# A planner's constants and a written order, both replaced: one core, a linear-attention block beside a ReLU block

## The chip, the cores and the metric

The kernel runs on one core of one Trainium2 chip. The metric is the time of one execution on the device in microseconds (us), and lower is better. A kernel is run several times and the median counts. Beside it stands one profiled execution, whose records are the source of every row of a view shown here.

## What is computed

The input `x` has 2048 rows (tokens) of 640 numbers in bfloat16. Its rows are normalised, and the normalised rows go into two branches that meet in a product at the end.

```
xn = layernorm(x)
q, k, v = xn @ wqkv                     # wqkv 640 x 1920, 32 heads of 20
phi(t) = where(t > 0, t + 1, exp(t)) + 1e-6
kv = einsum("bhsd,bhse->bhde", phi(k), v);  z = sum over s of phi(k)
s  = (phi(q) kv) / (phi(q) z) @ wo      # wo 640 x 640
g  = silu(relu(xn @ w1) @ w2)           # w1 640 x 1728, w2 1728 x 640
out = x + s * g
```

## The kernel before

**Tiles.** The 2048 tokens are 16 tiles of 128. A tile of `x` is 128 x 640; `x_load` (L562) brings one in with 160 KB. The weights of the keys `wk` come in five pieces of 160 KB, one for each 128 rows (`wk_load`, L586), and `w1` in seven pieces, six of them of 320 KB (`w1_load`, L582), the query weights in one load of 800 KB (L567).

**The head.** For the tiles 0 to 3 the rows are centred on VectorE (L695, L699) and turned by TensorE against an identity (L706), copied out of PSUM (L716, L718), and multiplied by `wk` (`K_mm`, L733, two halves of 320 columns times five pieces, ten matmuls a tile). For the tiles 4 to 7 and again 0 to 3 the normalised rows (`bn`, L637, `aggr`, L641, the power on GpSimd, L645, `LN_norm`, L673) are turned by transfers: `xnT_dma` (L722) issues one transposing DMA for a tile on SP's queue. Blocks of `w1` for tokens 0 to 511 (`P4`, `P5`, `P10`, `P11`, L823, five matmuls of 512 columns each) need only what TensorE turned. The key tiles 4 to 7 (`KT4` to `KT7`) and the blocks `H14`, `H15`, `H110`, `H111` need the turned tiles 4 to 7.

**The units.** Nearly all other products are done in Strassen-like units of seven steps, s1 to s7, of two or three matmuls each (L1164 in the first two thirds, L991 in the rest). A unit's right sides are sums of turned tiles that VectorE makes. `T0` makes the five for tiles 0 to 7: `hTv[1]`, `hTv[3]`, `hTv[2]`, `hTv[4]` and `x4d`; each waits for all eight transposing transfers. The unit `a0` is the first to use them: `a0.s1` needs the eight turned tiles, `a0.s5` also `hTv[1]`, `a0.s6` also `hTv[2]`, and `a0.s7` also that VectorE has read the PSUM bank of `a0.s6` (the addition L936 with psT on both sides). Elementwise VectorE work of all kinds goes through one helper, `tt` (L936).

**Order.** `PROGRAM` is a text of words; each word is a step, and its place gives TensorE's and SP's order for certain. For the part ahead of the sign `|` (the head) it gives the order of every engine. After it, `Sched.place` picks for VectorE, ScalarE and GpSimd, from the next 60 operations of each, by the times that its own cost rules give. The constants `lags` are two delays that these rules add to the DMA queue, each as (time from which it counts, length). Waits are semaphores, put where one engine needs another's result. Words that the text uses: `lx5` loads tile 5, `lk12` loads piece 1 of `wk`, `lw4` loads piece 4 of `w1`, and `wb` is `w1` piece 4 as well; `S4` and `N4` are the statistics and the norm of tile 4 with its transposing transfer; `k012` multiplies tile 0 by piece 1 of `wk`; `tr3` turns tile 3; `pf3` is a filler matmul; `rb` is a scaling with one transposing transfer (L1051); `xa`, `xb`, `xc`, `lx8` load two tiles each, `lq` the query weights.

Of the kernel before, what the change touches and what calls it, by code (L numbers as in the profile page):

```python
# [95 lines left out]
class Sched:  # L96
# [90 lines left out]
    def place(self):  # L187
        recs = self.recs
        queue = {E: [o for o in recs if o.E == E] for E in ENGS}
        for o in recs:  # L190
            o.succ = []
        for o in recs:
            for d in o.deps:
                recs[d].succ.append(o.n)
        t = sum(o.occ for o in queue["PE"]) + 10.0
        end = t + 4.0
        goal = {}
        for o in reversed(queue["PE"]):
            t -= o.occ
            goal[o.n] = t  # L200
        for o in reversed(recs):
            o.late = min([recs[s].late - o.dur - self.LAT[o.E] for s in o.succ] + [goal.get(o.n, end - o.dur)])
        free = {E: 0.8 for E in ENGS}
        line = 2.0
        lags = [(3.8, 0.6), (13.0, 0.7)]
        narrow = turned = False
        nleft = [len(o.deps) for o in recs]
        ready = [0.0] * len(recs)
        wait = {E: list(queue[E]) for E in ENGS}
        left = sum(len(w) for w in wait.values())  # L210
        while left:
            best = None
            for E in ENGS:
                w = wait[E]
                if not w:
                    continue
                if E in ("PE", "SP") or w[0].n < self.head:
                    c = w[0]
                    if nleft[c.n]:
                        continue  # L220
                    est = max(free[E], ready[c.n])
                else:
# [130 lines left out]
m0.s1 n13 n10 m0.s5 p1.s7 m0.s6 p1.s3 m0.s2 p1.s4 m0.s7 n14 m0.s3 Kb8 m0.s4 n15 a1.s1 a1.s5 Ka12 p0.s1 p0.s5 y3 a1.s6 a1.s2 p0.s6  # L353
a1.s7 Ka8 a1.s3 T1 a1.s4 p0.s3 F5 a2.s5 a2.s1 y0 y8 y4 hh0 a2.s6 a2.s2 p0.s7 Ka11 a2.s7 p0.s4 p0.s2 a2.s4 a2.s3 y7 y1
k1.s1 y5 k1.s5 b0.s1 y6 Kb12 b0.s5 k1.s6 b0.s6 ZS y12 b0.s2 k1.s7 k1.s3 b0.s7 k1.s2 k1.s4 Kb15 y13 b0.s4 q0.s1 b0.s3 q0.s5 b1.s1
q0.s6 b1.s5 q0.s2 b1.s6 q0.s7 y2 q0.s3 b1.s2 q0.s4 b1.s7 b1.s3 k2.s5 k2.s1 b1.s4 Kb11 k2.s6 y9 a3.s5 a3.s1 k2.s2 k2.s7 k2.s3 a3.s6 a3.s2
k2.s4 Ka15 y14 y15 a3.s7 q1.s5 w2a q1.s1 a3.s3 a3.s4 q1.s6 q1.s2 GS0 b2.s5 y10 b2.s1 q1.s7 q1.s3 b2.s6 b2.s2 y11 q1.s4 b2.s7 GT1
zm SH2 zs c0 b2.s4 b3.s1 b3.s5 b2.s3 m1.s1 b3.s6 b3.s2 m1.s5 m1.s6 b3.s7 m1.s2 b3.s3 m1.s7 m1.s3 b3.s4 c1 sl w2b b4.s1 b4.s5
m1.s4 b4.s6 b5.s5 b4.s2 b5.s1 b4.s7 b4.s3 zc b5.s6 GT2 b5.s2 b4.s4 b5.s7 b5.s3 g0.s1 GT3 b5.s4 g0.s5 wo g0.s6 w2c hh1 GT4 dn
w2d g0.s7 g0.s3 do0 g1.s1 GS1 g1.s5 rc0 do1 g1.s6 g1.s2 uT1 g0.s2 g1.s7 g0.s4 do3 g1.s3 wv1 uT3 g1.s4 u0.s1 wv0 uSa0 uSb0  # L360
uT2 kv1 uT4 dv0 kv0 u0.s5 u0.s6 rc1 W5 W4 do2 u0.s2 u0.s7 uSa2 W1 u0.s3 W3 u0.s4 W2 W0 uSa1 uSb2 xre uSb1
u1.s1 u2.s1 dv1 u1.s5 u1.s6 u2.s5 rc3 u2.s6 u1.s3 u1.s7 dv3 oT u2.s7 oS0 uSa3 u2.s3 u2.s2 u2.s4 u1.s4 o0.s5 o0.s1 rc2 u1.s2 u4.s1
o0.s6 uSa4 u4.s5 u4.s6 uSb4 o0.s2 dv2 o0.s7 o0.s3 u4.s7 uSb3 oS1 o0.s4 u4.s2 o1.s5 u4.s4 o1.s1 u4.s3 u3.s1 o1.s6 u3.s5 oS2 uSa6 u3.s6
o1.s2 o1.s7 o1.s3 u3.s7 o1.s4 o2.s5 u3.s3 o2.s1 uSa5 u3.s4 u3.s2 oS3 uSb5 o2.s6 u5.s1 u5.s5 o2.s7 u5.s6 o2.s2 o2.s3 oS4 o2.s4 u5.s7 uSa7
o3.s5 o3.s1 u5.s2 o3.s6 o3.s2 u5.s4 o3.s7 o3.s3 u5.s3 o4.s1 o3.s4 u6.s5 o4.s5 o4.s6 o4.s2 u6.s1 o4.s7 e3 oS5 o4.s3 uSb6 u6.s6 o4.s4 u6.s2
o5.s5 oS6 o5.s1 u6.s7 u6.s3 o5.s6 u6.s4 o5.s2 o5.s7 o5.s3 e0 uSb7 o6.s1 o5.s4 o6.s5 u7.s5 o6.s6 u7.s1 o6.s2 o6.s7 u7.s6 o6.s3 o6.s4 u7.s2
u7.s7 u7.s3 e1 f0 f3 f1 u7.s4 l0 l1
"""


# [1611 lines left out]
```

## Time and profile before

| what | value |
|---|---|
| median of 3 runs | 202.93 us (202.88 to 203.06) |
| the profiled execution, its own time | 202.67 us |
| its span (first to last instruction) | 201.4 us |
| TensorE busy | 197.4 us, 98% of the span |
| VectorE, ScalarE, GpSimd busy | 172.1, 131.8, 42.5 us |
| granted TensorE clock | 1.00 |

The profiled execution took 1.27 us more than its span, and its own time is 0.26 us under the median. A view's row for an engine has the start, the length, the engine, the line, the operation, what is written and read, and in brackets the idle time ahead of it with what ended it. PE is TensorE, PEld its weight loads, DVE VectorE, ACT ScalarE, POOL GpSimd, SPq the issuing of SP's transfers. A matmul of 512 columns that follows another without a wait starts 0.216 us after it, one of 320 columns 0.136 us. A few matmul records are missing in the trace, so a gap of exactly one such step is no wait.

### The profile page before, as it was taken

To read this page: it belongs to the slowest core of one execution; us is meant where nothing else is said; L and a number is where in the kernel's file an instruction comes from. 1 tells how busy PE (TensorE), PEld (TensorE's weight loads), DVE (VectorE), ACT (ScalarE), POOL (GpSimd) and SP (SyncE) were. 2 spreads that over 40 slices of the span, in tenths; PEclk is the share of its full clock that TensorE was granted. 3 is DMA by queue.
4 is the path that set the end of the run, shared out by engine and by line. 5 is a ranking of instruction groups with operands and counts; after the bars stand their busy time and mean duration, and the time that the engine had idled before them with its cause. 6 is when DMAs were issued, how large, how long until landed. Compare 5 with 4: busy or idle time off the path is not lost.

```text
span 201.4 us, 3628 instructions
## 1 busy us (share of the span) xinstructions
PE 197.4 (98%) x1302; PEld 120.5 (60%) x1312; DVE 172.1 (85%) x408; ACT 131.8 (65%) x279; POOL 42.5 (21%) x66
## 2 busy tenths in 40 slices
PE   8999999999999999999999999999999999999995
PEld 3756444554564464545555777777777777777774
DVE  5899799999999979999574999999969977686565
ACT  6889858998999998867933313471636354654533
POOL 3489504143345605542000000000000000000000
DMA  5999798245567986685406965995993010111104
GB/s 155 331 279 111 110 370 182 44 98 103 112 146 138 184 203 130 134 165 97 131 0 206 306 164 167 276 268 132 352 358 131 0 65 0 68 67 65 38 30 130
DMA packets 38487, 30.43 MB, mean 151 GB/s; under 512 B 13765, under 2 KB 38469, under 8 KB 38469
## 3 DMA queue, kind: packets, MB, share of 16 engines
q1 hardware_dynamic: 32885, 23.62, 43.0%
q0 software_dynamic: 4624, 5.57, 14.1%
q10 hardware_dynamic: 960, 1.02, 1.6%
q8 instruction: 10, 0.16, 0.4%
q14 instruction: 8, 0.07, 0.1%
HBM read 15.81 MB, written 5.24 MB: 105 GB/s over the span
## 4 chain that ended last, share of the span: by engine, by line
PE 94%; DVE 2%; DMA 1%; issue 1%; ACT 0%; DVEq 0%
PE psT L991 43%; PE psT L1164 33%; PE psT L733 6%; PE psT L823 3%; PE psT L1494 2%; PE psT L605 2%; DMA reg<-reg 1%; PE psT L1838 1%; PE psT L841 1%; PE psT L706 1%; PE psT L1629 1%; PE psT L1603 1%; DVE regH L936 1%; DVE reg L761 1%; PE psT L895 1%
## 5 line engine op out<-in xcount | busy, mean ns | idle before, releaser
L1164 PE MATMUL psT<-reg 128*128 128x512 bf16 (+2 forms) x160 | 43.2, 370 | 0.5 <-issue 0.2
L991 PE MATMUL psT<-reg,regH 128*128 128x320 bf16 (+1 forms) x224 | 34.3, 299 | 0.0
L991 PE MATMUL psT<-reg 128*128 128x320 bf16 (+1 forms) x178 | 28.7, 299 | 0.0
L991 PEld LDWEIGHTS psT<-reg,regH 128*128 128x128 bf16 (+1 forms) x224 | 21.9, 98 | 8.5
L1164 PEld LDWEIGHTS psT<-reg 128*128 128x128 bf16 (+1 forms) x166 | 15.9, 98 | 18.2 <-DVE psT L936 0.7
L863 POOL DMA_DIRECT2D regH<-reg x16 | 18.4, 1192 | 21.6 <-DMA regH<-reg 6.3
L991 PEld LDWEIGHTS psT<-reg 128*128 128x128 f16 (+1 forms) x178 | 17.4, 98 | 7.1
L998 ACT ACTIVATE reg<-psT 128x320 f32<-128x320 f32 (+1 forms) x24 | 10.4, 436 | 17.0 <-PE psT L991 15.8
L936 DVE TENSOR_TENSOR reg<-reg 128x1024 f16<-128x1024 bf16 (+11 forms) x30 | 18.8, 648 | 1.5 <-ACT reg L1853 1.0
L1214 ACT ACTIVATE regH<-psT 128x512 bf16<-128x512 f32 (+1 forms) x24 | 14.9, 620 | 3.3 <-PE psT L1164 3.1
L991 PE MATMUL psT<-reg,pqT 128*128 128x320 bf16 (+1 forms) x84 | 15.8, 299 | 0.0
L1665 ACT ACTIVATE wv_sb<-psT 128x320 bf16<-128x320 f32 (+2 forms) x21 | 8.8, 424 | 9.2 <-PE psT L991 8.1
L936 DVE TENSOR_TENSOR psT<-psT,reg 128x320 f32<-128x320 f32 (+1 forms) x21 | 11.4, 543 | 3.7 <-PE psT L991 3.5
L1853 ACT ACTIVATE reg<-psT 128x640 bf16<-128x640 f32 (+1 forms) x14 | 7.8, 568 | 10.1 <-PE psT L991 10.1
L637 DVE BATCH_NORM_STATS2 stats<-reg 128x6 f32<-128x320 bf16 x28 | 12.4, 483 | 1.7 <-DMA reg<-in_A_x_dram 1.7
L733 PE MATMUL psT<-reg 128*128 128x320 bf16 x80 | 12.3, 299 | 0.0
L1171 ACT ACTIVATE psT<-psT 128x512 f32<-128x512 f32 (+1 forms) x18 | 10.6, 599 | 1.6 <-PE psT L1164 1.5
L936 DVE TENSOR_TENSOR reg<-psT,reg 128x320 bf16<-128x320 f32 (+1 forms) x16 | 7.8, 488 | 4.5 <-PE psT L991 4.5
L800 ACT ACTIVATE regE<-psT 128x512 bf16<-128x512 f32 x16 | 9.7, 604 | 3.0 <-PE psT L1164 2.8
L936 DVE TENSOR_TENSOR psT<-psT,wv_sb 128x512 f32<-128x512 f32 (+1 forms) x14 | 9.2, 654 | 2.8 <-PE psT L1164 1.9
L998 ACT ACTIVATE psT<-psT 128x320 f32<-128x320 f32 x17 | 7.3, 429 | 5.9 <-PE psT L991 5.9
L733 PEld LDWEIGHTS psT<-reg 128*128 128x128 bf16 x80 | 7.8, 98 | 4.2
(173 smaller groups left out, 404.3 us busy)
## 6 DMA issues: line engine op xcount, KB each, us to landing
regH<-reg POOLq DMA_DIRECT2D x16, 320.0 KB, 3.6
reg<-in_B_w_dram SPq DMA_DIRECT2D x12, 320.0 KB, 5.0
scr<-rden SPq DMA_DIRECT2D x4, 640.0 KB, 6.0
reg<-in_A_x_dram SPq DMA_DIRECT2D x4, 640.0 KB, 6.3
out_dram<-reg SPq DMA_DIRECT2D x14, 160.0 KB, 1.8
regE<-scr SPq DMA_DIRECT2D x3, 640.0 KB, 8.8
reg<-in_A_x_dram SPq DMA_DIRECT2D x4, 320.0 KB, 5.7
reg<-in_A_x_dram SPq DMA_DIRECT2D x7, 160.0 KB, 3.8
```

The source lines that it names most:

```text
L637: sc.op("DVE", lambda eng: eng.bn_stats(stats[:, t, a, :], xv[:, HN * a:HN * (a + 1)]), R=[("xin", xs(t))], W=[("stats", t, a)])
L733: fns.append(lambda eng, a=a, k=k, lhs=lhs: eng.matmul(ps[bk[a]][:, 0:HN], lhsT=lhs, rhs=wk[:, k, HN * a:HN * (a + 1)], start=(k == 0), st ...
L800: exps.append(sc.op("ACT", lambda eng: eng.activation(out=e_, in_=src, func=ACTF.Exp), R=[key], W=[("er_e", es)]))
L863: dma("POOL", lambda eng: eng.dma_start(zacc[a], src, **kw), R=[key] + after, W=[("zacc", a)], chain=zchain[a])
L936: sc.op("DVE", lambda eng: eng.tensor_tensor(out=out, in0=in0, in1=in1, op=op), R=R, W=W, extra=extra)
L991: sc.group("PE", [(lambda eng, k=k, lhs=lhs, rhs=rhs: eng.matmul(ps[b][:, 0:HN], lhsT=lhs, rhs=rhs, start=(start and k == 0), stop=(k == n ...
L998: sc.op("ACT", lambda eng: eng.activation(out=dst, in_=ps[b][:, 0:HN], func=ACTF.Copy), R=[("ps", b)], W=[dkey], extra=extra)
L1164: sc.group("PE", [(lambda eng, k=k, lhs=lhs, rhs=rhs: eng.matmul(ps[b][:, 0:nn], lhsT=lhs if tile is None else rhs, rhs=rhs if tile is Non ...
L1171: sc.op("ACT", lambda eng: eng.activation(out=dst[:, 0:nn], in_=ps[b][:, 0:nn], func=ACTF.Copy), R=[("ps", b)], W=[dkey], extra=extra)
L1214: sc.op("ACT", lambda eng: eng.activation(out=dst, in_=ps[b], func=ACTF.Relu), R=[("ps", b)], W=[("hT", j, f)], extra=ex)
L1665: sc.op("ACT", lambda eng, lo=lo, hi=hi: eng.activation(out=g[:, lo:hi], in_=src[:, lo - HN * n:hi - HN * n], func=ACTF.Silu), R=[key, ("s ...
L1853: sc.op("ACT", lambda eng: eng.activation(out=o_[:, 0:n].rearrange("p (a n) -> p a n", a=2) if n == D else o_[:, 0:n], in_=src, func=ACTF. ...
```

## The change

The second constant of `lags` goes from 13.0 us and 0.7 us to 18.2 us and 1.2 us, the first from 3.8 us to 4.1 us, and `PROGRAM` is replaced by another order of the same words but for the key weights of the head (the same forty key matmuls cut into other pieces), the engine of single copies, and `wb`, which stands ahead of `|` now. No operation is added or taken away. The head and the first units of both:

```
-        lags = [(3.8, 0.6), (13.0, 0.7)]
+        lags = [(4.1, 0.6), (18.2, 1.2)]
...
-lx0 ba0 mh0 lx2 lk01 ax1 lk12 lx3 ma0 ce0 lk23 lk34 lx4 lk45 ma1 lx7 ce1 ma2 tr0 cd0 pf3 bb0 tr1 k001
-ce2 sq1 ma3 lx6 lx5 cd1 ca3 lw5 k012 lw2 cd2 tr2 k102 ca5 k023 ba3 ag0 mh3 k034 cd4 k123 ce3 S4 sq2
-lw3 lw0 S7 tr3 k134 k045 k201 ca7 N4 S5 k212 k145 N2 ca6 k301 S6 k225 N5 ke0 ke1 bb3 N7 k312 ag3
-k325 SH0_1 mv6 kr0 kr1 ke2 N6 kr2 P11 P5 P10 ke3 N1 kr3 N0 N3 lq |
-lx8 F0 F3 F1 P4 lw6 xb SH0_2 S8 xa wa rb KT4 F2 KT5 KT7 SK KT6 H110 wb n8 F4 H15 n12
-SQ F7 a0.s1 F6 T0 SM a0.s5 SH0_4 SH0_3 H111 a0.s6 n11 H14 SH1 a0.s2 a0.s7 xc n9 p1.s1 a0.s3 p1.s5 a0.s4 p1.s6 p1.s2
...
+lx0 ba0 ax1 lx2 ma0 mh0 lk01 ma1 lx3 ce0 lk12 bb0 lk23 lx4 ce1 lk34 lk45 lx7 lx5 lw5 ag0 lw2 lx6 lw3
+ma2 ce2 lw0 wb tr0 pf3 ca0 sq2 tr1 cd1 ba3 ma3 k001 cd2 cd3 mh3 S4 tr2 k012 k023 ce3 S7 k103 k034
+ca4 ca5 k045 sq1 ke0 N4 k202 N0 tr3 bb3 k224 S5 N7 S6 ca6 SH0_1 ca7 k245 k135 N5 kr0 ke1 kr1 F1
+ag3 N6 N1 ke2 kr2 k301 k315 N2 P11 P10 F0 P4 P5 N3 lx8 lq ke3 SH0_2 lw6 kr3 F2 |
+S8 xb xa SH0_4 KT4 n8 wa F3 KT5 SH0_3 n12 rb n11 xc KT7 n10 F4 n13 KT6 SH1 n9 n15 F7 n14
+H14 SQ H111 a0.s1 SM H110 T0 T1 SK y3 a0.s5 a0.s6 a0.s2 H15 p1.s1 a0.s7 p1.s5 a0.s3 p1.s6 a0.s4 p1.s2 m0.s5 F6 m0.s1
...
```

The order that comes of it, read off the built programs: SP issues eleven tile and key loads, then `w1` pieces 5 and 2, tile 6, pieces 3, 0 and 4, and then the eight transposing transfers for the tiles 4, 0, 7, 5, 6, 1, 2, 3; before, twelve such loads (tile 6 among them) and four pieces of `w1` stood ahead of the eight, which went in the order 4, 2, 5, 7, 6, 1, 0, 3. After the eight come `lx8` and `lq` (before: `lq` and `lx8`). VectorE's share of `T0` is made in the order `x4d`, `hTv[3]`, `hTv[1]`, `hTv[2]`, then the statistics of tile 8, then `hTv[4]`; before, it was `hTv[1]`, `hTv[3]`, one addition for the keys, `hTv[2]`. On TensorE the 106th matmul, counted from the start, is one of `KT5` in both.

More of the change, by code (lines that the diff above doesn't have):

```diff
@@ L353 @@
[L353 to L364, printed above, removed]
@@ L365 @@
-o3.s5 o3.s1 u5.s2 o3.s6 o3.s2 u5.s4 o3.s7 o3.s3 u5.s3 o4.s1 o3.s4 u6.s5 o4.s5 o4.s6 o4.s2 u6.s1 o4.s7 e3 oS5 o4.s3 uSb6 u6.s6 o4.s4 u6.s2
-o5.s5 oS6 o5.s1 u6.s7 u6.s3 o5.s6 u6.s4 o5.s2 o5.s7 o5.s3 e0 uSb7 o6.s1 o5.s4 o6.s5 u7.s5 o6.s6 u7.s1 o6.s2 o6.s7 u7.s6 o6.s3 o6.s4 u7.s2
-u7.s7 u7.s3 e1 f0 f3 f1 u7.s4 l0 l1
+lx0 ba0 ax1 lx2 ma0 mh0 lk01 ma1 lx3 ce0 lk12 bb0 lk23 lx4 ce1 lk34 lk45 lx7 lx5 lw5 ag0 lw2 lx6 lw3
+ma2 ce2 lw0 wb tr0 pf3 ca0 sq2 tr1 cd1 ba3 ma3 k001 cd2 cd3 mh3 S4 tr2 k012 k023 ce3 S7 k103 k034
@@ new lines @@
+ca4 ca5 k045 sq1 ke0 N4 k202 N0 tr3 bb3 k224 S5 N7 S6 ca6 SH0_1 ca7 k245 k135 N5 kr0 ke1 kr1 F1
+ag3 N6 N1 ke2 kr2 k301 k315 N2 P11 P10 F0 P4 P5 N3 lx8 lq ke3 SH0_2 lw6 kr3 F2 |
+S8 xb xa SH0_4 KT4 n8 wa F3 KT5 SH0_3 n12 rb n11 xc KT7 n10 F4 n13 KT6 SH1 n9 n15 F7 n14
+H14 SQ H111 a0.s1 SM H110 T0 T1 SK y3 a0.s5 a0.s6 a0.s2 H15 p1.s1 a0.s7 p1.s5 a0.s3 p1.s6 a0.s4 p1.s2 m0.s5 F6 m0.s1
+p1.s7 y4 Kb8 m0.s6 p1.s3 p1.s4 m0.s2 m0.s7 F5 y7 Ka8 y8 a1.s1 a1.s5 m0.s4 m0.s3 a1.s6 Ka12 ZS p0.s1 a1.s7 p0.s5 p0.s6 a1.s2
@@ new lines @@
+a1.s4 a1.s3 y0 p0.s3 a2.s1 p0.s7 a2.s5 a2.s6 y6 hh0 p0.s4 y5 a2.s2 a2.s7 y1 Ka11 p0.s2 a2.s4 k1.s1 a2.s3 mv6 k1.s5 b0.s1 y2
+Kb12 b0.s5 k1.s6 b0.s6 y12 b0.s2 k1.s7 k1.s2 b0.s7 k1.s4 k1.s3 b0.s3 b0.s4 q0.s1 Ka15 y13 q0.s5 b1.s1 q0.s6 b1.s5 q0.s2 b1.s6 q0.s7 q0.s3
+b1.s2 q0.s4 y9 b1.s7 b1.s3 k2.s5 k2.s1 b1.s4 Kb11 y11 k2.s6 a3.s5 a3.s1 k2.s2 k2.s3 k2.s7 a3.s6 a3.s2 k2.s4 Kb15 y15 y14 a3.s7 q1.s5
+q1.s1 a3.s3 a3.s4 y10 q1.s6 GS0 w2a q1.s2 b2.s5 b2.s1 q1.s7 q1.s3 zm b2.s6 b2.s2 q1.s4 b2.s7 SH2 c0 m1.s1 b2.s4 GT3 zs m1.s5
@@ new lines @@
+m1.s6 b2.s3 GT1 m1.s2 b3.s1 m1.s7 b3.s5 m1.s3 b3.s6 c1 b3.s7 m1.s4 b3.s3 b4.s5 b3.s4 b4.s1 b3.s2 b5.s5 GT2 b5.s1 b4.s6 zc b4.s2 b5.s6
+b4.s7 b5.s2 b4.s3 b4.s4 b5.s7 b5.s3 g0.s1 b5.s4 w2b g0.s5 g0.s6 hh1 wo w2d w2c dn g0.s3 g1.s1 GS1 g1.s5 g1.s6 sl GT4 do0
+uT3 g0.s7 g1.s2 g1.s7 rc0 g0.s2 uSa0 uT2 g1.s3 dv0 g0.s4 wv0 uT1 do2 do1 uSb0 g1.s4 u0.s1 u0.s5 wv1 kv1 u0.s6 W5 uSa2
+W4 kv0 do3 u0.s2 u0.s3 uT4 W3 W1 u0.s7 W2 uSa1 u1.s5 u1.s1 u0.s4 W0 uSb1 u1.s6 u2.s1 rc2 u2.s5 u1.s7 oT u2.s6 u1.s2
+u1.s3 uSb2 uSa4 rc1 u2.s7 oS0 u1.s4 u2.s2 dv1 u2.s4 uSa3 xre o0.s5 rc3 o0.s1 u2.s3 u4.s1 o0.s6 u4.s5 oS1 u4.s6 o0.s2 uSb4 o0.s7
@@ new lines @@
+o0.s3 dv3 u4.s7 o0.s4 oS2 u4.s3 o1.s5 o1.s1 u4.s4 u4.s2 o1.s6 u3.s1 u3.s5 o1.s7 uSa6 uSb3 u3.s6 o1.s2 o1.s3 o1.s4 u3.s7 o2.s1 u3.s2 oS3
+o2.s5 o2.s6 u3.s4 o2.s2 u3.s3 uSa5 o2.s7 o2.s3 u5.s1 o2.s4 u5.s5 dv2 o3.s5 o3.s1 u5.s6 u5.s2 o3.s6 uSb5 u5.s7 o3.s2 o3.s7 u5.s3 oS4 u5.s4
+o3.s3 uSb6 oS5 o3.s4 e3 o4.s1 o4.s5 u6.s5 o4.s6 u6.s1 o4.s2 o4.s7 o4.s3 oS6 u6.s6 o4.s4 u6.s2 o5.s5 o5.s1 u6.s7 u6.s3 o5.s6 u6.s4 o5.s2
+uSa7 o5.s7 o5.s3 o6.s1 e0 o5.s4 o6.s5 u7.s5 uSb7 o6.s6 u7.s1 o6.s2 o6.s7 o6.s3 u7.s6 o6.s4 u7.s2 u7.s7 f0 f3 e1 u7.s3 f1 u7.s4
@@ L368 @@
+l0 l1
 """
```

## The prediction

> **What bounds the kernel now.** I read the page first, then the busy time by stretches, the chain of waits, and the timelines of TensorE, SP and VectorE up to 29 us.
>
> ```profile
> span 201.4 us, 3628 instructions
> PE 197.4 (98%) x1302; PEld 120.5 (60%) x1312; DVE 172.1 (85%) x408; ACT 131.8 (65%) x279; POOL 42.5 (21%) x66
> PE 94%; DVE 2%; DMA 1%; issue 1%; ACT 0%; DVEq 0%
> 26.43:61.36 34.93, 34.58 (x189) 17.18 (x194) 34.77 (x96) 31.40 (x67) 12.11 (x21) 1.00 0.58 139
> 61.36:198.82 137.46, 137.25 (x966) 89.18 (x970) 114.64 (x247) 78.22 (x171) 14.78 (x13) 1.00 0.54 145
> 61.36 0.38 PE L1164 MATMUL psT<-reg 128*128 128x512 bf16 x1 [0.19 <-issue]
> ```
>
> TensorE is the bound: 98% busy, 94% of the chain. Of the two stretches after 26.43 us (length, then busy time of PE) the one idles 0.35 us and the other 0.21 us, and one missing record of 512 columns, 0.216 us, accounts for the second and most of the first. That leaves the row at 61.36 us: its 0.19 us of idle, and, against 60.80 us plus two steps of 0.216 us, a wait of 0.13 us. So an order can win next to nothing after 26.43 us, and can only lose there. What it can win lies before:
>
> ```profile
> 22.69 1.24 PE L823 MATMUL psT<-reg 128*128 128x512 bf16 x5
> 24.00 0.59 PE L1164 MATMUL psT<-reg 128*128 128x512 bf16 x2
> 24.74 0.60 PE L1164 MATMUL psT<-regE,pqT 128*128 128x512 f16 x2
> 25.18 1.24 PE L823 MATMUL psT<-reg 128*128 128x512 bf16 x5
> 26.43 0.59 PE L1164 MATMUL psT<-regX,pqT 128*128 128x512 f16 x2
> 60.80 0.38 PE L1164 MATMUL psT<-wv_sb,reg 128*128 128x512 f16 x1
> 21.23 2.68 DMA reg<-reg
> 23.99 0.69 DVE L936 TENSOR_TENSOR regE<-reg 128x1024 f16<-128x1024 bf16 x1 [1.00 <-DMA reg<-reg]
> ```
>
> These are TensorE's starts around `a0`. At 0.216 us a step it could have begun `a0.s1` at 22.69 + 1.08 = 23.77 us and began at 24.00; `a0.s5` at 24.43, began at 24.74; `a0.s6` at 26.26, began at 26.43. The three waits are 0.23, 0.31 and 0.17 us, 0.71 us in all. The chain's DMA row says where they are from: the last of the eight transposing transfers, issued at 21.23 us, landed at 21.23 + 2.68 = 23.91 us, and VectorE, idle for a microsecond, began `T0` on it at 23.99. All of `a0` hangs on that landing.
>
> **The transposing transfers (the first and largest term).** What sets the landing is SP's timeline and the queue's rows.
>
> ```profile
> 6.45 3.36 SPq L582 DMA_DIRECT2D reg<-in_B_w_dram  x4
> L582 SPq DMA_DIRECT2D reg<-in_B_w_dram x7: 434/526/1453, 6.5 to 28.8; - x7
> 10.64 1.33 SPq L722 DMA_TRANSPOSE reg<-reg  x1
> 15.96 2.60 SPq L722 DMA_TRANSPOSE reg<-reg  x2
> 17.29 3.90 SPq L722 DMA_TRANSPOSE reg<-reg  x2
> 21.23 1.27 SPq L722 DMA_TRANSPOSE reg<-reg  x1
> q8 instruction: 1, 0.02, 3.8%
> 0.00:18.43 18.43, 17.55 (x105) 10.14 (x107) 15.24 (x48) 15.27 (x32) 11.29 (x31) 1.00 0.87 232
> GB/s 155 331 279 111 110 370 182 44 98 103 112 146 138 184 203 130 134 165 97 131 0 206 306 164 167 276 268 132 352 358 131 0 65 0 68 67 65 38 30 130
> 10.16 0.45 DVE L673 TENSOR_SCALAR reg<-reg,mv,rsy 128x640 bf16<-128x640 bf16 x1
> ```
>
> SP hands out one such transfer every 1.3 us (2.60 us for two), so eight take about 9.2 us from the first issue to the last. One pair takes 3.90 us, 1.30 more, and in the 2.8 us from 18.4 us on the queue view has one packet of 0.02 MB on the instruction queue, the first since the program began. So the landing is: first issue 10.64 + 9.24 + 1.35 lost + 2.68 = 23.91 us.
>
> The Trainium skill ("Runtime: NRT & Kernel Launch", section "Instruction fetch mechanics") says that an engine's instructions come in blocks of 16 KiB, 256 at a time, and that crossing a block is mostly hidden. TensorE shows no wait there, so for its own sequencer the trace agrees; for the queue beside it the 1.30 us of the pair disagree, and the measurement decides.
>
> The read can't be planned away by this change: it comes after 105 recorded matmuls, and the 106th is one of `KT5` in both orders, at a time when transposing transfers are still being handed out. I keep the loss at 1.35 us in both, with 0.3 us to either side, since it depends on which of a transfer's packets it hits.
>
> What moves is the first issue. Two things hold it. VectorE must have made the norm of tile 4: before at 10.16 to 10.61 us, after the statistics of tile 7. In the new order tile 4 arrives one place earlier and tile 7 in the same place, so these statistics start some 0.2 us earlier (they need not queue behind tile 4's), and the norm ends at about 10.3 us: 0.3 us earlier is the low end. The other is SP. It issued four pieces of `w1` in 3.36 us, where a short issue is 0.434 us and the longest took 1.453: the queue was full, and an issue ended when something had drained. It ended at 6.45 + 3.36 = 9.81 us, 0.83 us ahead of the first transposing one. The new order puts a fifth piece in between. 320 KB (327,680 bytes) drain in 1.07 us at some 305 GB/s, the mean of the second and third slice of the GB/s row (331 and 279, 5 to 15 us). So SP is free at 9.81 + 1.07 = 10.88, and the first issue comes at about 10.92 us, 0.28 us later than before. The high end has a row too:
>
> ```profile
> 25.87 2.84 SPq L1051 DMA_TRANSPOSE wv_sb<-spx  x1
> ```
>
> This transposing transfer was issued behind six loads and its issue alone took 2.84 us, 1.51 more than the 1.33 of the row at 10.64. If the first of the eight fares a third to two thirds as badly behind its longer line, that is 0.5 to 1.0 us more. I take +0.28 us, the term for which every number is a row of the same place, and keep -0.3 and +1.2 as ends.
>
> **The key phase of the head.** TensorE waits for pieces of `wk` in it.
>
> ```profile
> 6.12 0.11 PEld L733 LDWEIGHTS psT<-reg,regX 128*128 128x128 bf16 x2 [0.21 <-DMA reg<-in_A_wqkv_dram]
> 6.53 0.49 DVE L637 BATCH_NORM_STATS2 stats<-reg 128x6 f32<-128x320 bf16 x1 [0.28 <-DMA reg<-in_A_x_dram]
> 8.04 0.89 DVE L637 BATCH_NORM_STATS2 stats<-reg 128x6 f32<-128x320 bf16 x2 [0.21 <-DMA reg<-in_A_x_dram]
> 8.33 3.69 PE L733 MATMUL psT<-reg,regX 128*128 128x320 bf16 x26
> ```
>
> Piece 1 lands just before 6.12 us, tile 3 before 6.53, and three loads later tile 4 before 8.04, 0.50 us each. The new order gives tile 3 the place of piece 1 and tile 4 that of piece 3, so piece 3 lands at about 8.0 and piece 4 in its old place at 8.5 us. TensorE can't go on with `k045` before; with it and after it come 26 matmuls of 0.136 us, and the turning of tile 3, 0.28 us: 8.5 + 3.53 + 0.28 = 12.3 us, against 8.33 + 3.53 = 11.86 now. That is 0.44 us, and it is covered: up to `a0.s1` lie the same 30 matmuls of 512 columns and 40 of 320 in both, 11.9 us, so TensorE arrives at 24.2 instead of 23.77 us, and the landing, 23.91 + 0.28 = 24.19 us, is as late. Cost nothing; but it spends the cover. If the landing came early, 24.2 us would be the bound.
>
> **From the landing to `a0.s7`.** Here VectorE's order changes.
>
> ```profile
> 24.60 0.69 DVE L936 TENSOR_TENSOR regX<-reg 128x1024 f16<-128x1024 bf16 x1
> 26.20 0.42 DVE L936 TENSOR_TENSOR regX<-reg,pqT 128x512 f16<-128x512 bf16 x1
> 26.54 0.69 DVE L936 TENSOR_TENSOR regE<-reg,regX 128x1024 f16<-128x1024 bf16 x1
> 27.47 0.70 DVE L936 TENSOR_TENSOR psT<-psT,wv_sb 128x512 f32<-128x512 f32 x1
> 9.08 0.83 DVE L637 BATCH_NORM_STATS2 stats<-reg 128x6 f32<-128x320 bf16 x2
> ```
>
> Steps from start to start: 1024 elements 0.61 us (23.99 to 24.60), 512 elements 0.34 (26.20 to 26.54), a statistic 0.41. Counted from `T0`'s start D: `x4d` 0.34, `hTv[3]` and `hTv[1]` to 1.56, `hTv[2]` done at 1.56 + 0.69 = 2.25; before, it was done at 26.29, D + 2.30. So `a0.s6` can't start much before D + 2.4, as now (26.43 is D + 2.44), and the block of `H110` in the wait hides no more than that of `H111` did. Then come two statistics of tile 8, `hTv[4]`, about 0.8 us of small work with another statistic, and the addition that frees the bank for `a0.s7`: 2.17 + 0.82 + 0.61 + 0.8 = 4.4, done at D + 5.1. TensorE with no wait after `a0.s6` gets to `a0.s7` at 2.44 + 0.43 + 0.65 + 1.08 + 0.43 = D + 5.03. Before, the addition ended at 28.17 us and `a0.s7` came after it with room. So a wait of 0.1 us to 0.3 (should tile 8's load keep VectorE) is new; I take 0.15.
>
> **The rest.** Moves of the units, of copies, and of `wb` out of the later queue cost nothing as far as I can price them: TensorE hides them, with the waits gone or at 0.13 us. But VectorE is busy for 34.77 of the 34.93 us from 26.43 to 61.36, so a unit that moves up has nothing to lean on there. I put this at 0, from -0.13 (the wait at 61.36 gone) to +0.5 us (three or four waits of the size of that one).
>
> **The sum.** +0.28 (first issue) + 0.15 (`a0.s7`) + 0 = +0.43 us. On the profiled execution: 202.67 + 0.43 = 203.10 us. That execution lies 0.26 us under the median of the runs, 202.93, so on the scale of the medians it is 203.36, rounded to 203.4 us.
>
> **The rivals.**
>
> *The landing comes earlier (faster).* The queue doesn't hold SP at the fifth piece, the first issue follows the norm at 10.34 us, 0.3 earlier, or the instruction read falls into a pause between two transfers. Then TensorE is the bound, at 24.2 us for `a0.s1`; of the 0.71 us of waits 0.43 are spent in the key phase, and 0.3 us are won, 0.13 more if the wait at 61.36 us goes, and 0.6 in all if the key phase loses less than I think. For it: the norm is earlier. Against it: the 1.453 us issue. Time 202.3 to 202.6 us.
>
> *The first transposing issue is stretched (clearly slower).* Behind a full queue it takes 1.0 us longer, as the row of 2.84 us suggests. It decides from the point where the last landing passes 24.3 us, TensorE's arrival. Price +1.2 us with the rest: 204.1 us.
>
> *Nothing moves.* The landing stays within 0.1 us, since tile 6's load now stands between the pieces and leaves SP less held, and VectorE's order costs nothing: 202.8 to 203.1 us.
>
> *The middle gives way.* VectorE, full up to 61 us, makes new waits for the units: +0.5 us on top of the forecast, 203.9 us.
>
> **How the numbers follow.** About 0.2% (0.4 us) is what a measurement of this kernel can tell from no change. The forecast, slower by 0.2 to 0.6 us, gets 0.32; the stretched issue 0.13 and the middle 0.11; nothing moves 0.16; the early landing 0.28. The forecast's case reaches into "within 0.2%" with about a fifth of its chance, the early landing with 0.04 of its 0.28, which gives faster 0.26, same 0.22, slower 0.52. The range from 202.3 to 204.3 us takes in the ends of the first issue and of the middle.
>
> **What would show it right or wrong.** In the profile of the changed kernel: the first transposing issue at about 10.9 us behind five pieces of `w1` (wrong if at 10.4; the stretched case if its own length passes 1.8 us); one pair at 3.9 us beside an instruction packet; VectorE's first addition of `T0` near 24.3 us; the `P` blocks starting at about 12.3 us; a short wait of TensorE at `a0.s7` behind VectorE; no wait over 0.3 us after 30 us. A start of `a0.s6` before 26.3 us would make the forecast wrong.

## The result and the profile after

Six runs of the changed kernel have a median of 205.23 us (204.09 to 206.09), beside 202.91 us (202.52 to 203.37) for six of the kernel before on the same chip: a ratio of 1.0112, with 95% interval 1.0075 to 1.015. The change costs 2.3 us, where 0.43 was forecast; the time lies above the range. The profiled execution took 206.09 us, the slowest of the six, so its trace shows more loss than the median has.

From the page of the changed kernel: its span, TensorE's row, and the shares of the chain that ended last.

```profile
span 204.8 us, 3631 instructions
PE 199.0 (97%) x1312; PEld 119.2 (58%) x1312; DVE 172.6 (84%) x407; ACT 132.5 (65%) x280; POOL 37.7 (18%) x66
PE 76%; DVE 7%; DMA 6%; ACT 5%; SPq 3%; issue 2%; POOL 1%; DVEq 0%
```

TensorE's busy time is 1.6 us more than before, with ten more matmul records of the same work. Its share of the chain has gone from 94% to 76%: DMA, VectorE, ScalarE and SP's queue now hold stretches that were TensorE's own. (The chain runs along them also where TensorE is busy beside them; the lost time itself is read from TensorE's waits below.)

SP's timeline around the first transposing transfers (start, length, engine, line):

```profile
7.96 3.29 SPq L582 DMA_DIRECT2D reg<-in_B_w_dram  x3
10.27 0.99 SPq L582 DMA_DIRECT2D reg<-in_B_w_dram  x1
11.30 2.59 SPq L722 DMA_TRANSPOSE reg<-reg  x1
13.94 1.26 SPq L722 DMA_TRANSPOSE reg<-reg  x1
```

The first issue comes at 11.30 us, not 10.92, and takes 2.59 us, where the prediction put the mark of the stretched case at 1.8. The second starts at 13.94 us; before it started at 12.02. The chain has the last of the eight, TensorE's timeline what hangs on it:

```profile
21.86 4.09 DMA reg<-reg
```

```profile
19.34 4.23 PE L733 MATMUL psT<-reg 128*128 128x320 bf16 x30 [0.58 <-DMA reg<-reg]
26.04 0.59 PE L1164 MATMUL psT<-reg 128*128 128x512 bf16 x2 [0.30 <-DMA reg<-reg]
28.35 0.59 PE L1164 MATMUL psT<-regX,pqT 128*128 128x512 f16 x2
144.46 0.72 PE L991 MATMUL psT<-reg,regH 128*128 128x320 f16 x4 [0.89 <-DVE psT L936]
```

The last landing is at 21.86 + 4.09 = 25.95 us (23.91 before), `a0.s1` starts at 26.04 (24.00) and `a0.s6` at 28.35 (26.43): 1.92 us are lost by then. The row at 19.34 is new: `KT5` waits for tile 5, which is now transposed fourth and not third. So is the row at 144.46, which no step of the prediction has. The chain shows how it comes about:

```profile
137.72 0.50 SPq L1644
138.26 2.02 SPq L1644
140.33 2.74 DMA reg<-reg
143.51 0.48 DVE reg L936
143.99 0.42 DVE psT L936
144.46 0.58 PE psT L991 x3
```

L1644 stores the pieces of `wf`; the last lands at 143.07 us. VectorE's next instructions are the first two of `oT`, which need all of `wf`, and the addition that frees TensorE's bank stands behind them.

From `a0.s6` to the end of the last matmul the traces give 172.66 us before and 174.16 after. Of the 1.50 more, 1.05 are the wait that ends at 144.46 us. The other 0.45 are mainly short waits between 40 and 57 us (0.08, 0.12, 0.21 and 0.10 in the trace's steps), with the 0.13 us at 61 us gone.

### The profile page after: what moved, and what is told of

Same layout as the page of the kernel before. It is cut to its first block, busy times and chain, and to the rows that moved or that the text cites. A ratio compares the mean times of both kernels' runs of the same rounds, so it can differ in the third digit from the quotient of the medians.

```text
span 204.8 us, 3631 instructions
## 1 busy us (share of the span) xinstructions
PE 199.0 (97%) x1312; PEld 119.2 (58%) x1312; DVE 172.6 (84%) x407; ACT 132.5 (65%) x280; POOL 37.7 (18%) x66
## 4 chain that ended last, share of the span: by engine, by line
PE 76%; DVE 7%; DMA 6%; ACT 5%; SPq 3%; issue 2%; POOL 1%; DVEq 0%
PE psT L991 39%; PE psT L1164 26%; PE psT L733 4%; DMA reg<-reg 3%; DMA reg<-in_A_wqkv_dram 2%; PE psT L1494 2%; ACT pqT L802 1%; DVE stats L637 1%; SPq L1644 1%; PE psT L1838 1%; PE psT L841 1%; PE psT L823 1%; DVE reg L936 1%; ACT regE L800 1%; ACT regE L743 1%
## 5 line engine op out<-in xcount | busy, mean ns | idle before, releaser
L1164 PE MATMUL psT<-reg 128*128 128x512 bf16 (+2 forms) x166 | 44.7, 370 | 0.3 <-DMA reg<-reg 0.3
L1164 PEld LDWEIGHTS psT<-reg 128*128 128x128 bf16 (+1 forms) x166 | 15.8, 98 | 18.0 <-DVE psT L936 0.9
```

The costliest lines, as they stand in the source:

```text
L1164: sc.group("PE", [(lambda eng, k=k, lhs=lhs, rhs=rhs: eng.matmul(ps[b][:, 0:nn], lhsT=lhs if tile is None else rhs, rhs=rhs if tile is Non ...
```

## The experiments

Most edits move single records of the planner's order and leave every other engine's order as it is. They use one helper, at the end of the file:

```python
def moved(seq, recs, moves):
    for a, b in moves:  # record a goes right behind record b
        seq.remove(recs[a])
        seq.insert(seq.index(recs[b]) + 1, recs[a])
    return seq
```

All their results in one table. The landings, the start of `a0.s6` and the rest (from there to the end of the last matmul) are read from the trace of the profiled execution, in us; "last copy" is the latest landing among the loads that are issued ahead of the transposing ones. "Fifth piece" is the piece of `w1` that the change puts ahead of them.

| kernel | last copy | first / last transposed | a0.s6 | rest | this execution | median |
|---|---|---|---|---|---|---|
| before | 14.26 | 14.98 / 23.91 | 26.43 | 172.66 | 202.67 | 202.91 |
| before, again | 15.31 | 16.03 / 24.76 | 27.29 | 172.67 | 203.51 | 203.00 |
| after | 16.24 | 16.80 / 25.95 | 28.35 | 174.16 | 206.09 | 205.23 |
| after, fifth piece back | 15.30 | 15.99 / 25.55 | 27.95 | 173.10 | 204.63 | 204.37 |
| after, oT behind | 16.19 | 16.75 / 25.78 | 28.19 | 173.09 | 204.86 | 205.06 |
| before, fifth piece ahead | 16.38 | 17.11 / 26.17 | 28.70 | 172.66 | 204.90 | 204.06 |
| after, key loads as before | 16.38 | 16.95 / 25.56 | 27.96 | 173.24 | 204.75 | 204.95 |
| before, two pieces by ScalarE | 15.24 | 15.94 / 24.68 | 27.21 | 172.67 | 203.58 | 203.37 |
| after, fifth piece by ScalarE | 15.43 | 16.14 / 25.59 | 27.98 | 174.21 | 205.74 | 205.68 |
| both repairs | 15.06 | 15.76 / 25.31 | 27.71 | 173.10 | 204.40 | 204.58 |
| both, and norm 5 first | 14.60 | 15.28 / 24.31 | 26.71 | 173.31 | 203.58 | 203.83 |

The two mixtures and the kernel with early waits, further below, aren't in it. Three things hold in every row. The first transposed tile lands 0.56 to 0.73 us behind the last copy. `a0.s6` starts 2.39 to 2.53 us behind the last transposed tile. And the execution's time is `a0.s6` plus the rest plus 3.5 to 3.7 us. So only two numbers have to be explained: the landing, and the rest.

**One piece of w1.** The fifth piece is put back in the changed kernel, behind the next piece of `w1` in the later queue:

```diff
-        seq = self.place()
+        seq = moved(self.place(), self.recs, ((40, 160),))
```

> The changed kernel with one move: the fifth piece of w1 goes from ahead of the eight transposing transfers to behind the load of tiles 10 and 11 and the next piece of w1, in the later queue; every other engine's order stays. If the fifth piece holds SP's first transposing issue (the queue theory): that issue comes at about 10.3 us instead of 11.30 and takes 1.3 us instead of 2.59, the last landing falls from 25.95 us to about 23.9, a0.s1 is then bound by the P blocks at 13.04 + 11.9 = 24.95 us instead of 26.04, and the time falls by 1.0 to 1.2 us, not by the whole 2 us. If the key phase alone makes the delay: the landing falls as well, but the time stays within 0.2 us. If the 2.59 us have another cause than the queue, the first issue stays at 2.5 us or so and the time falls by 0.3 us at most.

Measured: 204.37 us (204.04 to 204.96), 1.0071 of before [1.005, 1.0091], 0.86 us less than the changed kernel. SP's timeline, and VectorE's:

```profile
10.73 2.11 SPq L722 DMA_TRANSPOSE reg<-reg  x1
```

```profile
15.49 0.42 DVE L936 TENSOR_TENSOR pqT<-reg 128x512 f16<-128x512 bf16 x1 [0.91 <-ACT regH L827]
15.83 0.44 DVE L673 TENSOR_SCALAR reg<-reg,mv,rsy 128x640 bf16<-128x640 bf16 x1
```

The last copy lands 0.94 us earlier and the first transposed tile 0.81, as the queue theory has it. But the first issue still takes 2.11 us and not 1.3, the last landing gains only 0.40 us and not 2, and the median falls by less than the 1.0 to 1.2 us written down. Nor is all of the 0.86 us the head's: this trace lacks the wait at 143 us, which belongs to the column "rest". Where both kernels have `oT` moved (205.06 us, and 204.58 with both repairs, below), the medians differ by 0.48 us and the means by 0.8. So the piece put back is worth some 0.5 to 0.9 us. The fourth issue comes at 16.30 us in this trace, 0.8 us after SP is free: it waits for the norm of tile 5 (the row at 15.83), which stands behind an addition of two pieces of `w1` (`SH0_1`, at 15.49). This second bound, hidden as long as the copies are later, is taken up in the last experiment.

The mirror image, in the kernel before:

```diff
-        seq = self.place()
+        seq = moved(self.place(), self.recs, ((185, 73),))
```

> The kernel before with one move: the same piece of w1 goes ahead of its eight transposing transfers; every other engine's order stays. Queue theory: first transposing issue at about 10.9 to 11.3 us and 2.5 us long, landing near 25.8 instead of 23.91 us, a0.s6 at 28.2 instead of 26.43, time slower by 1.5 to 2.0 us. The prediction's own term: issue at 10.92 with its usual 1.33 us, landing 24.19, slower by 0.3 us. If it is the new key order that delays the queue: less than 0.3 us.

Measured: 204.06 us (203.65 to 204.9), 1.0062 [1.0037, 1.0086], 1.10 us more than before, with nothing else moved on any engine.

```profile
6.45 5.42 SPq L582 DMA_DIRECT2D reg<-in_B_w_dram  x5
11.91 2.32 SPq L722 DMA_TRANSPOSE reg<-reg  x1
```

The first issue is at 11.91 us and 2.32 long. The prediction's own term (0.3 us) is refuted. So is the size that the queue theory had here, 1.5 to 2.0 us: two single profiles lie that far apart, the medians don't. Put ahead with nothing else changed, the piece costs 1.10 us, about the 1.07 us that it takes to drain.

**The kernel before once more.** Is the stretched issue the new order's alone?

> The kernel before, unchanged, for a second profile of its head. In the first profile the sixteen DMA engines ended each early piece of w1 within 0.2 us of each other's last ones; in every kernel with the fifth piece ahead, and in the one with it put back, one or two engines ended 0.7 to 1.4 us after the others, and the transposing transfers waited for them. If this lag belongs to the new order: none here, last landing near 23.9 us again. If it comes and goes with each execution: a lag of 0.5 us or more can show here too, with the last piece of w1 landing at 14.8 us or later instead of 14.26 and a0.s6 after 26.8 us instead of 26.43.

Measured: 203.0 us (202.28 to 204.05), 0.9998 [0.9976, 1.0021]. SP's timeline, then the chain, of this second profile:

```profile
11.06 1.75 SPq L722 DMA_TRANSPOSE reg<-reg  x1
```

```profile
8.46 6.84 DMA reg<-in_B_w_dram
22.08 2.68 DMA reg<-reg
```

It is not. The same program now has its last piece of `w1` landing at 8.46 + 6.84 = 15.30 us, a first issue of 1.75 us, and the last landing at 24.76. What differs is how evenly the sixteen DMA engines run: each transfer leaves sixteen marks, and for the first piece of `w1` that is issued the last mark comes 0.70 us behind the median one in the first profile (not within 0.2, as it was written down), 1.22 in this one, and 1.56 in the changed kernel's. The GB/s row of the 4 us from 13 us on, in 40 slices, shows what this does; before, before again, and after:

```profile
GB/s 284 264 266 282 259 218 192 133 125 82 41 238 260 294 294 287 279 267 254 276 276 266 223 236 101 18 0 0 8 97 228 212 212 233 200 207 190 49 3 0
```

```profile
GB/s 271 302 292 282 287 279 277 287 284 269 251 202 179 159 102 74 69 54 54 49 20 90 260 287 289 289 289 271 260 287 287 294 292 246 127 3 0 23 131 187
```

```profile
GB/s 312 266 307 282 287 297 287 292 282 292 284 292 264 282 269 241 215 166 123 79 51 46 41 38 38 38 33 18 20 87 260 287 292 289 289 264 247 274 266 259
```

Between the copies and the transposing transfers lies a hole: short in the first profile (13.6 to 14.1 us), about a microsecond in the others. In it the packets of the first transposing transfer stand for up to 1.0 us (before) and 1.7 us (after) until the slowest engine has finished its copies. The profile on which the prediction stood was an even execution: by `a0.s6` the same program can be 0.86 us later.

Over the eleven profiles of the table this lag goes from 0.41 to 1.77 us. Sorted by it, the column "last copy" comes apart into two effects that add up:

| lag of the first piece | four pieces ahead | five pieces ahead |
|---|---|---|
| 0.4 to 0.7 us | 14.26, 14.60 | 15.43 |
| 1.2 to 1.3 us | 15.06, 15.31 | none |
| 1.5 to 1.8 us | 15.24, 15.30 | 16.19, 16.24, 16.38, 16.38 |

With engines equally even, the fifth piece makes the last copy some 1.0 us later, which is its drain; and an uneven execution makes it some 0.6 to 1.0 us later, with either number of pieces.

**Which queue?** Two of the four pieces of the kernel before go out by ScalarE's queue, at the same place in the order (the helper takes a fourth argument here, records that it hands to ScalarE with `recs[a].E = "ACT"`):

```diff
-        seq = self.place()
+        seq = moved(self.place(), self.recs, (), (72, 73))
```

> The kernel before with its third and fourth piece of w1 issued by ScalarE's queue instead of SP's, at the same place in time. If a transposing transfer waits for what stands ahead of it in its own queue: two pieces less ahead of the first one, its landing falls from 14.98 us to about 13.6, the last landing to about 23.0, the 0.71 us of waits around a0 shrink to 0.1 to 0.3, and the time falls by 0.4 to 0.6 us. If it waits for all that the DMA engines still hold, whatever queue it came by: the landing stays at 14.9 to 15.2 us, the time within 0.2 us, or up to 0.3 us slower for ScalarE's time at the issues.

Measured: 203.37 us (202.71 to 204.1), 1.0014 [0.9998, 1.0031]. The first transposed tile lands at 15.94 us, 0.70 behind the last copy, which came by the other queue, and 1.56 behind the last copy of SP's own (14.38). So waiting in its own queue isn't it: with that queue free the first issue has its usual length, and the landing is as late as in the second profile of the kernel before (16.03 us; the range written down, 14.9 to 15.2, came from the first).

```profile
10.93 1.32 SPq L722 DMA_TRANSPOSE reg<-reg  x1
```

The Trainium skill ("DMA: Bandwidth & Descriptors", section "Issuing engines are not separate DMA queues") says that transfers from several issuing engines run on the same sixteen DMA engines, so that spreading them saves issue time alone. The run agrees: the issue is shorter, the landing isn't earlier. ScalarE's time for the issues shows at the `P` blocks, without harm:

```profile
13.21 1.02 PE L823 MATMUL psT<-regX,reg 128*128 128x512 bf16 x4 [0.77 <-ACT regE L743]
```

The same with the fifth piece (record 40) of the changed kernel:

> The changed kernel with its fifth piece of w1 issued by ScalarE's queue instead of SP's. Own-queue theory: as if the piece were put back: first landing from 16.80 us to about 15.9, time faster by 0.7 to 1.0 us (the kernel with the piece put back took 204.37). All-engines theory: the landing stays at 16.6 to 16.9 us and the time within 0.3 us of the changed kernel's 205.23.

Measured: 205.68 us (205.23 to 206.69), 1.0132 [1.0098, 1.0167]: no gain. The first transposed tile landed at 16.14 us, near the own-queue forecast (15.9) rather than the other (16.6 to 16.9), so the landing alone would mislead. But this was the most even execution of all (a lag of 0.41 us), and in the small table its last copy, 15.43 us, lies where five pieces put it. The fourth issue waited for norm 5 here too (16.43 us), and the wait for `wf` was there (1.10 us).

**The key phase.** The loads of tiles 3 and 4 go back behind their pieces of `wk` (moves (18, 21) and (24, 26)).

> The changed kernel with the loads of x tiles 3 and 4 put back behind the pieces of wk as before (two moves in SP's queue, no other order changed). If the key phase lies under the landing, as the prediction had it: the P blocks start earlier than 13.04 us, by 0.4 to 1.2 us, the landing stays at 25.9 us, and the time stays within 0.2 us. If the key phase decides: the time falls by 0.4 to 1.0 us. If tile 4, now landing 0.5 us later, delays the first norm past SP's 11.26 us: slower by up to 0.3 us.

Measured: 204.95 us (204.65 to 207.53), 1.0117 [1.0077, 1.0156]. That is 0.28 us under the changed kernel, within the spread of either: no proof of a gain. Counting the one matmul record that is missing at its place, the `P` blocks start near 12.6 us. With the changed kernel's key order they start at 12.93 us where a piece of `wk` lands late, at 8.66 us (the profiled run), and at 12.25 to 12.6 in the five others: the loads put back don't start them earlier. In this kernel TensorE comes to `a0.s1` without a wait and still waits 0.25 us at `a0.s6`: the landing comes last.

**oT.** VectorE's first two subtractions of `oT` go behind the addition that they hold up (moves (849, 855) and (850, 849)).

> The changed kernel with one move: VectorE's first two subtractions of oT, which wait for the last piece of wf, go one place back, behind the addition that frees the bank of u2.s7's successor. If VectorE's order makes the wait of 1.05 us at 143.27: the wait goes, the time falls by 0.6 to 1.05 us, and the single times lie within 1 us of each other instead of 2. Rival: the late landing of wf itself holds what comes next (o0.s5 needs oT), and the wait comes back at the first o0 step: time within 0.2 us.

Measured: 205.06 us (204.86 to 206.27), 1.012 [1.0094, 1.0146]. No wait at 143 us in the trace, but the median is only 0.17 lower, and the single times still spread over 1.4 us. Why: the wait is not in every execution. The instruction queue's row of the DMA view, 136 to 144 us, for the changed kernel and for the one with the key loads put back:

```profile
q8 instruction: 1, 0.02, 1.2%
```

```profile
q8 instruction: 1, 0.02, 0.7%
```

A block of TensorE's instructions is read in the midst of the pieces of `wf`. Where it took 1.6 us (1.2% of sixteen engines over 8 us) or 1.7 us (the kernel with the piece on ScalarE's queue), one issue took 2.0 to 2.2 us instead of 0.83 and TensorE waited 1.05 and 1.10 us. Where it took 0.92 us, with the same order of VectorE, TensorE didn't wait there (key loads put back; fifth piece put back). In this kernel's own trace it took 0.92 us as well, so that trace doesn't show whether the move removes the wait. The last kernel below, which has the same move, does: there the read took 1.40 us, one issue 1.95, and `wf` landed 114.5 us behind `a0.s6`, nearly as late as in the two traces with the wait (114.7 and 114.8; 113.5 here). TensorE waited 0.21 us, later on, instead of 1.05.

**What lies behind the head.** A mixture: the words of the kernel before up to `KT4`, those of the changed kernel behind.

> A mixture: the order of the kernel before up to the first block of KT4, that of the changed kernel behind it, with the words that the one has earlier than the other put where they fit (the fifth piece of w1 behind KT6). If what the change costs behind the head is its own order (waits of 0.08 to 0.21 us between 40 and 57 us, 0.4 us in all): slower than before by 0.3 to 0.5 us, 203.3 us. If those waits only follow from the late head: within 0.2 us of before. If the new order behind the head holds more than the traces showed: slower by 0.7 us or more.

Measured: 208.87 us, 1.0282 [1.024, 1.0325]. The fifth piece had ended up behind six transposing transfers and landed too late; TensorE's timeline shows the wait, some 3 of the 5.9 us lost (L1162 here is L1164 elsewhere). In the ten us behind it the granted clock is 0.87, and its mean over this run is 0.991, where every other profiled run has 1.00.

```profile
49.79 1.03 PE L1162 MATMUL psT<-reg 128*128 128x512 bf16 x2 [2.96 <-DMA reg<-in_B_w_dram]
```

> The mixture again, with the fifth piece of w1 where the kernel before loads it, right behind the row scaling, since in the first mixture TensorE waited 3.1 us at 46.45 us for that piece, which was loaded behind six transposing transfers. If the order behind the head costs 0.43 us (from a0.s6 to the end 173.09 us in place of 172.66) and 1.05 us more in about half of the executions (the wait for wf): 203.0 + 0.43 + 0.5 = 203.9 us, with single times between 203 and 205. If those costs belong to the late head only: 203.0 us. If the planner makes another order of VectorE behind this head: anything up to 205.

Measured, with the piece loaded in time: 205.14 us (204.55 to 205.79), 1.0104 [1.0085, 1.0122]. `a0.s6` starts at 26.01 us, and the rest takes 175.55: behind another head the planner makes another order of VectorE, with longer waits for it.

```profile
34.58 0.58 PE L733 MATMUL psT<-reg 128*128 128x320 bf16 x3 [0.65 <-DMA reg<-reg]
46.03 0.60 PE L1164 MATMUL psT<-regE,reg 128*128 128x512 f16 x2 [0.41 <-DVE regH L936]
55.05 0.60 PE L1164 MATMUL psT<-regE,reg 128*128 128x512 f16 x2 [0.39 <-DVE regH L936]
```

So the mixture doesn't isolate the 0.43 us. What stands for it is the column "rest": 172.66 or 172.67 in all four profiles with the old order behind the head (and 172.67 in the next experiment, whose head is 7 us late), and at least 173.09 in all seven with the new one. That a late head makes these waits is thereby ruled out; which of the moved words makes them was not tested.

**The read of instructions.** In the kernel before, waits that are already met stand between the eight filling matmuls, so that the block of instructions ends sooner (the 23 waits in the text become 11 instructions of TensorE, most with two waits each):

```diff
-    (lambda eng, w=w: eng.matmul(...))
+    (lambda eng, w=w: ([eng.wait_ge(done_sems["DVE"], 1) for _ in range(23 if n == 32 else 0)], eng.matmul(...))[1])
```

> The kernel before with 88 waits that are already met, put between TensorE's eight filling matmuls while it has nothing to do, so that it reaches the end of its block of instructions some 44 matmuls earlier. If the read of instructions costs what the gap between the fifth and sixth landing shows (3.76 us for 1.32 in two profiles, less 1.1 us that the last two landings catch up: 1.34 us): the read comes at about 11 us, in the copies, the eight landings follow each other by 1.3 us throughout, and the last one comes 9.45 - 1.34 = 8.1 us behind the last copy. The read then holds one of the sixteen DMA engines during the copies, so the last copy lands 0 to 1 us later: time faster by 0.2 to 0.7 us, since TensorE's own arrival is next, 0.7 us below. Rival: the read costs as much there as it did (the last copy lands 1.3 us later): time within 0.2 us. Other rival: the waits themselves delay TensorE's first work past 4.4 us by more than 0.3 us: slower.

Measured: 209.83 us, 1.0328 [1.031, 1.0346]: the second rival. TensorE's timeline:

```profile
3.39 0.58 PE L605 MATMUL psT<-const-bfloat16-1.0 128*128 128x512 bf16 x1 [0.64 <-issue]
4.58 0.59 PE L605 MATMUL psT<-const-bfloat16-1.0 128*128 128x512 bf16 x1 [0.60 <-DVE reg L699]
```

Matmuls that had followed each other by 0.43 us now do so by 1.2, and TensorE's first real work comes 6.6 us late. As a bid for time it failed. It still measures something: the copies are all done (14.73 us) and the read is over (it starts at 15.94 us and takes 1.0) before the first issue at 17.07. It came 2.5 us earlier than in the kernel before, while all else came later, so the reads of the queue q8 belong to TensorE's instructions.

```profile
17.07 10.56 SPq L722 DMA_TRANSPOSE reg<-reg  x8
```

Eight issues take 10.56 us, 1.32 each, and the first tile lands 2.72 us after its issue, against 4.34 before and 5.50 in the changed kernel. The first seven landings follow each other by 1.30 to 1.33 us. In the changed kernel the last three landings take 4.09 us from the first of them to the last, where two steps of 1.32 make 2.64: 1.45 us are lost, and by the same count 1.34 in the kernel before and 0.90 to 1.71 in the other rows of the table.

But more than the one read lies in these stretches. In the kernel before, the queue view of 18.4 to 21.2 us, on which the prediction rests, has two rows of instructions:

```profile
q8 instruction: 1, 0.02, 3.8%
q14 instruction: 1, 0.01, 0.7%
```

The second read, 8 KB at 20.98 us, is in the changed kernel too (23.82 us), among the last landings. Here it comes at 28.46 us, between the seventh landing and the eighth, and the eighth is 2.18 us behind the seventh, 0.86 more than a step. The next load was issued at 27.67 us, so it may have a share in that. What the 16 KB read costs by itself is therefore not shown: the 1.34 and 1.45 us are the price of all that comes between, and 1.3 us a step is what the transfers do with neither read among them.

**Both repairs, and a third.** The fifth piece put back and `oT` one place later:

> The changed kernel with both repairs: the fifth piece of w1 put back and oT one place later on VectorE. Sum of the terms: 203.0 of before, + 0.43 for the middle, + 0.5 to 0.8 for the norm of tile 5, on which SP waits once the copies are out of its way, + 0 for wf: 203.9 to 204.3 us, with a0.s6 at 27.9 us, 173.09 us from there to the end, and no wait at 143 us. If the two repairs overlap: 204.4, as the first alone.

Measured: 204.58 us (204.4 to 204.77), 1.0079 [1.0065, 1.0093]. The rest is 173.10, there is no wait at 143 us in the trace (the read took 0.92 us), and single times lie within 0.4 us. But the median is no better than with the piece alone, and the head (27.71 us against 27.95) hardly. VectorE's timeline, and SP's:

```profile
15.25 0.42 DVE L936 TENSOR_TENSOR pqT<-reg 128x512 f16<-128x512 bf16 x1 [0.92 <-DMA reg<-in_B_w_dram]
15.59 0.44 DVE L673 TENSOR_SCALAR reg<-reg,mv,rsy 128x640 bf16<-128x640 bf16 x1
```

```profile
16.06 1.20 SPq L722 DMA_TRANSPOSE reg<-reg  x1
```

`SH0_1` waits for a piece of `w1`, the norm of tile 5 stands behind it, and SP's fourth issue behind that. One more move, (103, 107), lets the norm go first:

> The kernel with both repairs and one more move: VectorE's norm of tile 5 goes ahead of its first addition of two pieces of w1 (SH0_1), which waits for the last copy. In the kernel with both repairs VectorE stood idle for 0.92 us ahead of that addition, the norm behind it began at 15.59 us and SP issued the fourth transposing transfer at 16.06 instead of some 15.3 us. If that wait is what was left of the head's loss: fourth issue at 15.2 to 15.4 us, last landing 9.5 instead of 10.25 us behind the last copy, a0.s6 at about 27.0 instead of 27.71, time 203.8 to 203.9 us (204.58 - 0.7), which leaves the 0.43 us behind the head against before, and another 0.4 at most. Rival: the transposing queue makes up for the late issue anyway (it has two transfers in flight): last landing 10.0 us or more behind the last copy, time within 0.2 us of 204.58.

Measured: 203.83 us (203.33 to 204.9), 1.0047 [1.0025, 1.0069], 0.75 us less, as written down. (The two were measured on two chips; against the kernel before on the same chip the gain is 0.65 us by the ratios and 0.95 by the medians.) VectorE's timeline, then the chain:

```profile
13.69 0.39 DVE L673 TENSOR_SCALAR reg<-reg,mv,rsy 128x640 bf16<-128x640 bf16 x1
14.79 0.42 DVE L936 TENSOR_TENSOR pqT<-reg 128x512 f16<-128x512 bf16 x1 [0.71 <-DMA reg<-in_B_w_dram]
```

```profile
21.43 2.89 DMA reg<-reg
```

The last tile lands 9.71 us behind the last copy instead of 10.25. The trace is also of an even execution (a lag of 0.60 us, against 1.32 with both repairs), which by itself moves the last copy; the 0.54 us less behind it are the norm's. Three repairs of an order that is otherwise the changed kernel's take back 1.4 of its 2.3 us. What is left, 0.7 us over the 203.12 us of the kernel before beside it, is mostly the rest (173.31 for 172.66). No version here beats the kernel before.

## Why the prediction was wrong

**The bound** was read rightly: in every row of the table `a0.s6` follows the last landing by 2.4 to 2.5 us, and behind it no order gained anything.

**The first issue (+0.28 us): mis-sized, and the first step that failed.** The prediction took SP as what holds the first transposing transfer, saw it free 0.83 us ahead of the norm, and let the fifth piece fill that gap. SP did hold the first issue, but until 11.26 us and not 10.88; the issue then took 2.59 us, and the second one came 1.92 us later than before. The pieces of `w1` land 4.6 to 6.7 us after their issue in the two traces. What holds the transposing transfers is the draining of all copies ahead, by whichever queue, and a gap in SP's time covers nothing of it. The piece alone, put ahead in the kernel before, cost 1.10 us, against 1.07 for its drain; taken back it gave 0.5 to 0.9, since the norm of tile 5 then holds SP. The rival of the stretched issue came about; its cause isn't the line in SP's queue (the run with two pieces by ScalarE) but the copies still under way, down to those of the slowest DMA engine. A full queue only makes it visible as a long issue, and it does so in the kernel before as well (1.75 us in its second profile).

**The baseline.** A start at 10.64 us and an issue of 1.33 were taken as the kernel's; they were one even execution's. The shift of 0.26 us to the median covers only part of what the second profile showed.

**The instruction read (1.35 us in both, 0.3 to either side)** held as a size, 1.34 and 1.45 us in the two profiles, and not as a reading: the view had a second read in the same 2.8 us, so the loss isn't shown to be the first one's. Nor did the read come at a fixed place: after 116 recorded matmuls in the changed kernel, not 105. The Trainium skill's rule on it ("Runtime: NRT & Kernel Launch", section "Instruction fetch mechanics"), that the crossing of a block is mostly hidden, agrees with TensorE in the traces of both kernels, which shows no wait at this read (18.43 and 21.63 us); it doesn't speak of the transfers beside the read.

**The key phase (`P` blocks at 12.3 us, covered)** held. The start was 12.25 to 12.6 us in the kernels with the changed key order, 12.93 in the profiled run, and in all of them `a0.s6` still waits 0.25 us for VectorE behind the landing. That tile 5 comes fourth and `KT5` waits for it was not seen; it is covered too.

**The wait at `a0.s7` (+0.15 us)** is not in the trace of the changed kernel: the addition that frees the bank was done 4.92 us behind `T0`'s start and not 5.1, just ahead of TensorE (4.96). The step failed by its whole size.

**The rest (0, from -0.13 to +0.5 us): the second step that failed.** It was 0.43 us and not 0. The rival "the middle gives way" came about near its price, together with the stretched issue instead of in place of it. The wait for `wf`, 1.05 us in two of the four profiles that have `oT` in the changed order, was not looked for at all: "TensorE hides them" was said of all copies, without asking where VectorE meets the DMAs behind `W0`.

The sum from the table: `a0.s6` 28.27 us (mean of the two profiles with the changed head) against 26.86 (mean of two before) makes 1.41; the rest 0.43; together 1.84 of the 2.3 us. The wait for `wf` can fill what is left. Its share in the median isn't settled, since moving `oT` alone lowered the median by no more than the spread.

**The chances** don't add up as told: by the text's own shares the five cases give faster 0.24, same 0.26 and slower 0.50, not 0.26, 0.22 and 0.52. That the change would be slower was forecast, but the path to it was another one: the terms of the forecast hold a first issue 0.28 us later and a wait at `a0.s7`, and neither is what cost the time.

## What to carry to other kernels

Ahead of a transposing transfer count the bytes that the DMA engines still hold, by all queues, not the idle time of the engine that issues: one more load ahead cost its whole drain here (1.10 us for 320 KB). When an order is picked anew, look behind every instruction that waits for a DMA for what its engine does next; both waits found late here (`SH0_1` ahead of a norm, `oT` ahead of an addition) are of that kind. When a forecast is about a few tenths, take a second profile of the kernel before first: a head that lives on DMA landings moved by 0.86 us between two executions of one program.

## What the runs showed of the hardware

- The first of these transposing transfers lands only when the copies ahead are done, on the slowest of the sixteen DMA engines and by whichever queue. In all eleven profiles of the table it landed 0.56 to 0.73 us after the last copy; with the copies done, in one more, 2.72 us after its issue. While it waits the core moves some 20 to 50 GB/s instead of 290.
- That the engines run apart isn't tied to an order: the last one ended the first piece of `w1` 0.70 and 1.22 us behind the median in two executions of one program, and 0.41 to 1.77 over all. What makes them differ stays open.
- A read of TensorE's instructions (one packet of 16 KB) doesn't take the same time in each execution. In the eleven profiles the one at 135 to 139 us took 0.92 us in seven and 1.4 to 1.7 in four; the issue beside it took up to 1.44 us in the seven and 1.76 to 2.21 in the four. Which of the two makes the other long isn't shown.
- Waits that are already met aren't free: 11 wait instructions between two filling matmuls added 0.8 us to their distance.
